# Attention and gated products on one core: chunks of 384 tokens instead of 256 from the second sequence on

## The chip, the core and the metric

The kernel runs on one core of one Trainium2 chip. The metric is the device time of one execution in microseconds (us), launch to end. Before the change three executions took 678.44, 678.51 and 681.38 us; their median is 678.51.

## The reference

Inputs are q, k and v of shape (4, 8, 768, 64), that is 4 sequences, 8 heads, 768 tokens and 64 columns, and three weights. Attention looks at the tokens nearer than 16 and at one summary for each block of 32 tokens; what it gives goes through two products whose results are multiplied, and a third.

```python
k_sum = k.reshape(B, H, nb, 32, D).max(axis=3)
v_sum = v.reshape(B, H, nb, 32, D).mean(axis=3)
scores_l = np.where(abs(i - j) < 16, scale * q @ k.T, -1e9)
scores_s = scale * q @ k_sum.T + np.log(32)
a = softmax(concatenate([scores_l, scores_s]))
x = (a @ concatenate([v, v_sum])).reshape(3072, 512)
out = ((x @ w_a) * (x @ w_b)) @ w_out        # 512 -> 1536 -> 512, all float32
```

## The kernel before

**Tiling.** The 3072 tokens are cut into 12 chunks of 256 (CH), three to a sequence. The 1536 hidden columns are cut into 12 slices f of 128. An *item* is one slice for one chunk: 24 up products (12 for "a" into one half of a bank, 12 for "b" into the other; 4 pieces of 128 rows times three hi/lo parts, since each float32 operand is held as a high and a low part of type fp32r), a chain that forms a times b and splits it, and 6 down products of 128x512 that add into two output banks. The chain of an item is: ACT copies "a" to g (L1013), DVE multiplies into the bank (L1016), ACT casts to the high part gh (L1018), DVE subtracts for the low part gl (L1021). Items alternate between banks h0 and h1 and between two copies of g, gh and gl. The down products with gh and gl of an item (L1070, L1071) are ranked half an item after its up products, so they stand in PE's order behind the up products of the next item.

**Stages.** Chunks 0 and 1 run side by side while the weights are loaded and converted; that part has its own attention code (`first_attention`). FILL is 2: the attention of chunk 2 is made during that stage. From there on one chunk after the other runs through its 12 items, and the attention of chunk u+2 is put in behind the last item of chunk u, so that it is made while PE works on chunk u+1. Attention goes by tiles of 128 queries: 32 score products into two banks, then on DVE scale and mask (L642), maxima and sums, on ACT the exponentials (L662), on GpSimd (POOL) the division, 12 transposes of 32x32 blocks on DVE (L736), 32 value products (L750), and a split of the result into the chunk's inputs x hi (ACT, L758) and x lo (DVE, L761). There is one score buffer `s`, one transposed buffer `pt` and one pair of value windows vw0, vw1. From chunk 4 on a tile's value products are held back (`lead`) and stand in front of the next tile's scores. The first chunk of each later sequence also brings `prep_keys` (keys transposed, block maxima) and `prep_values` (block means by GpSimd, which go through a part of S0 into the value windows).

**Order.** Nothing is put on an engine as it is written. Each step is given to `Work` with an engine, a rank, an estimated time and the names that it reads and writes; `emit` then plays the program through by these estimates, and on each engine takes the ready step of the lowest rank. The chain's steps have rank 0 (CHAIN), attention of the later chunks rank 6 (LATER), PE's attention products rank -1, loads about 100 on SP's queue. The table ORDER shifts some of the first 626 steps by their number; the change leaves it as it is.

**Banks and buffers.** h0, h1: up products. o0, o1: output of even and odd rows of a chunk (o2, o3 for chunk 1). c0, c1, and o2, o3 in turn: scores and values. At the end of a chunk ACT copies o0 and DVE copies o1 into S0 (L1076, L1082), and SP sends each to DRAM. In names of rows, numbers behind an underscore are only serial numbers of buffers.

## Time and profile before

| | |
|---|---|
| median of 3 executions | 678.51 us |
| the profiled execution, its own time | 678.28 us |
| its span in the trace | 676.5 us |
| mean granted clock of TensorE | 0.999 |
| L736, block transposes on DVE into `pt` | 228, busy 99.4 us |

The profile is of one execution. "Busy" is the time in which an engine has an instruction under way; PE is the matrix engine's products and PEld its weight loads, which run beside them. A group's row gives line, engine, operation, output and inputs, shape, count, then busy time and the mean duration of one in ns, then the idle time in front of such instructions and what ended it. A timeline row gives the start, the duration from the first to the last of a run of like instructions, the engine, the line and, in brackets, the wait and its releaser. SPq is the time in which SP issues transfers; DMA rows are the transfers themselves.

### The profile page before, as it was taken

How to read it: one execution, taken by the hardware profiler on the slowest of the kernel's cores; microseconds unless marked ns; L12 is line 12 of the kernel's file. 1: busy time of each engine (PE TensorE's matmuls, PEld its weight loads, DVE VectorE, ACT ScalarE, POOL GpSimd, SP SyncE). 2: the span in 40 equal slices, each digit the busy share in tenths (PEclk: the TensorE clock that was granted, in tenths of full speed). 3: DMA queues.
4: the chain of work that ended last, by engine and by line, in shares of the span. 5: the costliest groups of instructions: out<-in, count | busy, mean ns of one | idle time of the engine just before them, and what ended most of it. 6: DMA issues, size and time to landing. Idle time of an engine off the chain costs nothing.

```text
span 676.5 us, 15121 instructions
## 1 busy us (share of the span) xinstructions
PE 657.0 (97%) x5988; PEld 620.7 (92%) x5988; DVE 434.4 (64%) x989; ACT 255.4 (38%) x797; POOL 186.8 (28%) x231
## 2 busy tenths in 40 slices
PE   6889999999999999999999999999999999999997
PEld 4679989899999999999999999999999999999996
DVE  4799999996757768777665776762772762322222
ACT  4996665533323333234332332332332432211211
POOL 6678979851533310413110101110110110000000
PEclk9999999999999999999999999999999999999999
DMA  9999863266224135532311330310310100000000
GB/s 226 264 284 238 266 169 126 41 137 137 67 78 112 49 56 103 96 61 80 57 25 28 75 57 15 77 25 1 87 25 1 56 22 1 33 1 1 32 1 32
DMA packets 155087, 54.84 MB, mean 81 GB/s; under 512 B 132472, under 2 KB 148088, under 8 KB 155016
## 3 DMA queue, kind: packets, MB, share of 16 engines
q1 hardware_dynamic: 154872, 53.74, 33.5%
q8 instruction: 47, 0.77, 0.5%
q14 instruction: 24, 0.20, 0.1%
q10 hardware_dynamic: 144, 0.13, 0.1%
HBM read 47.12 MB, written 6.29 MB: 79 GB/s over the span
## 4 chain that ended last, share of the span: by engine, by line
PE 77%; DVE 11%; SPq 3%; ACT 3%; issue 2%; DMA 2%; POOL 1%; DVEq 0%; ACTq 0%; POOLq 0%
PE h L987 47%; PE o L1031 23%; SPq L260 3%; DVE c L339 2%; PE c L750 2%; PE c L617 2%; PE o L750 1%; DVE pt L736 1%; ACT s L662 1%; DVE space L345 1%; PE o L617 1%; DVE S L345 1%; DVE space L332 1%; DMA space<-in_v_dram 1%; DVE S L332 1%
## 5 line engine op out<-in xcount | busy, mean ns | idle before, releaser
L987 PEld LDWEIGHTS h<-x,w 128*128 128x128 f32 x3456 | 405.0, 192 | 6.8 <-DVE x L761 0.6
L987 PE MATMUL h<-x,w 128*128 128x256 f32 x3456 | 406.7, 275 | 0.3 <-DVE x L761 0.3
L1016 DVE TENSOR_TENSOR h<-h,g 128x256 f32<-128x256 f32 x144 | 61.9, 430 | 148.9 <-ACT g L1013 147.6
L1031 PE MATMUL o<-w,gh 128*128 128x512 f32 x576 | 151.8, 386 | 1.4 <-ACT gh L1018 1.3
L1013 ACT COPY g<-h 128x256 f32<-128x256 f32 x144 | 53.6, 372 | 256.4 <-PE h L987 256.3
L1031 PEld LDWEIGHTS o<-w,gh 128*128 128x128 f32 x576 | 103.6, 197 | 12.1 <-ACT gh L1018 2.6
L692 POOL TENSOR_TENSOR s<-s,nml 128x512 f32<-128x512 f32 x40 | 41.6, 1041 | 233.1 <-DVE nml L677 232.6
L736 DVE STREAM_TRANSPOSE pt<-s 32x256 f32<-32x256 f32 x228 | 99.4, 436 | 7.1 <-POOL s L692 2.0
L1031 PE MATMUL o<-w,gl 128*128 128x512 f32 x288 | 86.3, 381 | 0.0
L1021 DVE TENSOR_TENSOR gl<-h,gh 128x256 fp32r<-128x256 f32 x144 | 60.4, 419 | 30.6 <-ACT gh L1018 29.3
L662 ACT ACTIVATE s<-s,nml 128x128 f32<-128x128 f32 x160 | 62.2, 391 | 44.9 <-DVE nml L650 44.9
L1018 ACT CAST gh<-h 128x256 fp32r<-128x256 f32 x144 | 53.5, 371 | 65.3 <-DVE h L1016 65.1
L1031 PEld LDWEIGHTS o<-w,gl 128*128 128x128 f32 x288 | 55.9, 196 | 6.1 <-issue 0.3
L545 POOL TENSOR_TENSOR S<-S 96x64 f32<-96x64 f32 (+3 forms) x54 | 35.2, 651 | 41.6 <-DMA S<-in_v_dram 30.7
L324 ACT ACTIVATE c<-raw 128x512 f32<-128x512 f32 x36 | 26.9, 748 | 13.1 <-DVE S L332 6.6
L662 ACT ACTIVATION_READ_ACCUMULATOR s<-s,nml 128x1 f32 x160 | 30.1, 188 | 0.0
L382 POOL TENSOR_TENSOR space<-space,w 128x1024 f32<-128x1024 f32 (+1 forms) x14 | 26.8, 1915 | 8.8 <-ACT w L377 6.6
L671 DVE TENSOR_SCALAR nml<-nml 128x4 f32<-128x4 f32 x40 | 9.6, 243 | 28.4 <-ACT s L662 28.4
L388 POOL TENSOR_TENSOR w<-space 128x1024 fp32r<-128x1024 f32 (+1 forms) x14 | 26.7, 1912 | 1.0
L650 DVE TENSOR_REDUCE nml<-s 128x4 f32<-128x512 f32 x40 | 25.3, 667 | 0.0
L444 POOL COPY kT<-ksum 128x144 f32<-128x144 f32 x16 | 4.7, 308 | 62.8 <-DVE ksum L522 48.0
L382 POOL TENSOR_TENSOR S<-S,w 128x512 f32<-128x512 f32 (+1 forms) x11 | 17.4, 1582 | 6.4 <-ACT w L377 6.4
(109 smaller groups left out, 460.6 us busy)
## 6 DMA issues: line engine op xcount, KB each, us to landing
raw<-in_moe_w_a_dram SPq DMA_DIRECT2D x12, 512.0 KB
raw<-in_moe_w_b_dram SPq DMA_DIRECT2D x12, 512.0 KB
raw<-in_moe_w_out_dram SPq DMA_DIRECT2D x12, 512.0 KB
out_dram<-S SPq DMA_DIRECT2D x23, 256.0 KB
qin<-in_q_dram SPq DMA_DIRECT2D x160, 32.0 KB
S<-in_v_dram SPq DMA_DIRECT2D x24, 192.0 KB
vw<-in_v_dram SPq DMA_DIRECT2D x18, 192.0 KB
kin<-in_k_dram SPq DMA_DIRECT2D x24, 100.0 KB
```

The costliest lines, as they stand in the source:

```text
L324: nc.scalar.activation(bank["c0"], high[:, :, 1].bitcast(F32), AF.Prelu, scale=2.0**-112, alpha=-(2.0**32))
L382: lambda ms=ms, f8=f8: nc.gpsimd.tensor_tensor(out=f8, in0=f8, in1=parted(0)[:, ms].bitcast(F32), op=ALU.subtract),
L545: lambda: nc.gpsimd.tensor_tensor(out=out, in0=i0, in1=i1, op=ALU.add),
L662: lambda h=h, c=c, sums=sums: nc.scalar.activation(s[h][:, c, :], x[h][:, c, :], AF.Exp, bias=m[:, 0, h, c : c + 1], scale=1.0, accum_out= ...
L692: lambda h=h, r=r: nc.gpsimd.tensor_tensor(out=s[h], in0=s[h], in1=r[:, :, None].broadcast_to([P, NP, P]), op=ALU.mult,),
L736: lambda js=js, qs=qs: nc.vector.transpose(out=pv[js, :, qs], in_=sv[qs, :, js]),
L987: nc.tensor.matmul(ps, w[:, c, part, :], x[xpart][:, c, :].rearrange("p (a b) -> p b a", a=G), start=(i == 0), stop=(i == n - 1),)
L1013: act(CHAIN, 0.38, [hk], [gk], lambda: nc.scalar.copy(out=g, in_=pa))
L1016: lambda: nc.vector.tensor_tensor(out=pa, in0=pb, in1=g, op=ALU.mult),
L1018: act(CHAIN, 0.41, [hk], [ghk], lambda: nc.scalar.copy(out=gh, in_=pa))
L1021: lambda: nc.vector.tensor_tensor(out=gl, in0=pa, in1=gh.bitcast(F32), op=ALU.subtract),
L1031: nc.tensor.matmul(bank[ok[j]], (gh if first else gl)[:, j::G], w[:, :, part, :].rearrange("p (z a) n -> p z n a", a=2), start=(f == 0 and ...
```

## The change

Sequence 0 keeps its three chunks of 256 tokens. The other three sequences are cut into two chunks of 384 each (`WIDE` = 3 tiles of 128), so there are 9 chunks and 108 items in place of 144; 36 of the items are those of chunks 0 to 2 and 72 are wide. With it go:

- From chunk 2 on "a" has bank h0 and "b" bank h1, each up to 384 columns wide, and there is one g, gh and gl of 384 columns. Chunks 0 and 1 keep the old item.
- The down products of a wide item are nine, into o0, o1 and o2. Value products go to o3, scores always to c0 and c1.
- All chunks' inputs lie in one tile `x` of nine pieces; the low part of chunk 3 lies in `late`, in S0's place. Tokens within a piece are read in an order that takes one from each half of 64 in turn.
- Output copies go through two pieces of S1 in place of S0; the third bank's copy uses the first piece again.
- Queries are loaded tile by tile (16 loads of 32x4x32 each) in place of chunk by chunk. Block means go from `vm` straight into the value windows, 8 transfers for each of the two windows.
- Key rows of the second half go through the same buffer `kin` as those of the first, but for sequence 1.
- The last item's "b" products are ranked ahead of a part of the down products before.

```diff
+    WIDE = 3
+    chunks = [(0, t, G) for t in range(0, S // P, G)]
+    chunks += [(b, t, WIDE) for b in range(1, B) for t in range(0, S // P, WIDE)]
+    NU = len(chunks)
...
-    xs = [[sb([P, NP, CH], f"x{i}_{p}", F32R) for p in range(2)] for i in range(2)]
-    gs = [sb([P, CH], f"g{i}") for i in range(2)]
+    xt = sb([P, 9, NP, P], "x", F32R)
+    gt, ght, glt = sb([P, 2 * CH], "g"), sb([P, WIDE * P], "gh", F32R), sb([P, WIDE * P], "gl", F32R)
...
+    def homes_of(u):
+        n = chunks[u][2]
+        if u <= FILL:
+            return [[f"X{u % 2 * 2 * G + p * G + i}" for i in range(n)] for p in range(2)]
+        if u % 2:
+            return [[f"X{6 + i}" for i in range(n)], [f"S0.{i}" for i in range(n)]]
+        return [[f"X{p * WIDE + i}" for i in range(n)] for p in range(2)]
...
     def prep_keys(b):
-        more = ["done12"], ["S1.2", "S1.3"]
+        if b == 1:
+            work.add("-", 0, 0, 0, (), ["S0.0", "S0.1"], lambda: None)
         for c in range(NP):
-            kw = kins[c % 2]
+            own = b == 1 and c % 2
+            kw = spaces["S0"][:, : S + 32] if own else kin
...
     def prep_values(b):
-            for h in range(4):
-                load(
-                    99, 6.0, 20, [pk, vk], [f"{vk}.{hg}.{h}"],
-                    vs[:, 4 * hg + h, :], vm[h * NS : (h + 1) * NS, :],
-                )
...
         def split():
+            act(
+                CHAIN if u > FILL else rank, 0.6, [bk], [hk] + (also if i == 2 else []),
+                lambda: nc.scalar.copy(out=home(0), in_=y),
+            )
             dve(
-                rank, 0.6, [bk, xk + "h"], [xk + "l"],
+                CHAIN if u > FILL else rank, 0.6, [bk, hk], [lk] + (also if i == 0 else []),
...
     def attention(u):
-        if u > FILL:
-            banks, vbank = [["c0", "c1"], ["o2", "o3"]], ["c0", "o2"]
+        banks, vbank = ["c0", "c1"], ["c0", "c1"] if u == FILL else ["o3"] * n
...
         def bring(i):
-                    load(97, 49.0, 100, sums, [VK[3 + e]], vbuf[e][r0 : r0 + NS], vsums[b])
+                    for h in range(H):
+                        load(
+                            97, 6.0, 20, [f"vm{h // 4}"],
+                            [f"v{3 + e}.{h}"] + [VK[3 + e]] * (u == FILL + 1),
+                            vbuf[e][r0 : r0 + NS, h, :],
+                            vm[h % 4 * NS : (h % 4 + 1) * NS, h // 4, :],
+                        )
         def begin(i):
+            if u > FILL:
+                for c in range(NP):
+                    keys += blocks(
+                        98, f"q{(t0 + i) % 2}.{c}", qin[:, c, place(i)], q, b, c, (t0 + i) * P, (),
+                        fill if u == FILL + 1 and i < 2 else (),
+                    )
...
     def up(nm, f, u, ps):
-                    x[xpart][:, c, :].rearrange("p (a b) -> p b a", a=G),
+                    inputs_of(u, xpart)[:, :, c].rearrange("p g (a b) -> p g b a", a=2),
...
     def item(n, u, f):
+        ok = [f"o{2 * (u == 1) + j}" for j in range(m)]
+            W = m * P
+            pa, pb, g, gh, gl = bank["h0"][:, :W], bank["h1"][:, :W], gt[:, :W], ght[:, :W], glt[:, :W]
+            for nm, ps, hk in (("a", pa, "h0"), ("b", pb, "h1")):
+                pe(
+                    n - (1.45 if n == total - 1 and nm == "b" else 0), 12 * (0.112 if m == 2 else 0.163), xk + weight_key(f, nm), [hk],
+                    lambda nm=nm, ps=ps: up(nm, f, u, ps),
+                )
+            act(CHAIN, 0.13 + W / 1030, ["h0"], ["g0", "g1"], lambda: nc.scalar.copy(out=g, in_=pa))
...
-                        bank[ok[j]], (gh if first else gl)[:, j::G],
+                        bank[ok[j]], (gh if first else gl)[:, j * P : (j + 1) * P],
...
         if f == NF - 1:
-            for j in range(2):
-                ob, key = slot("S0", j)
+            for j in range(m):
+                ob, key = slot("S1", j % 2)
```

Three places show how the order of the instructions changes. The first is **PE in the later chunks**. A row has the line, the operation, output and inputs, the shape, what it waits for, and a count; h are the up banks, o the output banks, x the inputs, w a piece of the weights. Before, around one run of down products:

```order
L987 MATMUL h0_75<-x1_0_171,w15_1477 128x256
L1031 MATMUL o0_71<-w14_1384,gh1_176 128x512 [waits Activation_49]
L1031 MATMUL o0_71<-w14_1384,gh1_176 128x512
L1031 MATMUL o1_72<-w14_1384,gh1_176 128x512 x2
L1031 MATMUL o0_71<-w14_1384,gl1_178 128x512 [waits DVE_49]
L1031 MATMUL o1_72<-w14_1384,gl1_178 128x512
L987 MATMUL h1_76<-x1_0_171,w16_1558 128x256
```

And now:

```order
L1024 MATMUL h1_76<-x_169,w5_802 128x384 x12
L1024 MATMUL h0_75<-x_169,w6_871 128x384 [waits Activation_49]
L1024 MATMUL h0_75<-x_169,w6_871 128x384 x11
L1095 MATMUL o0_71<-w5_802,gh_171 128x512 [waits Activation_49]
L1095 MATMUL o0_71<-w5_802,gh_171 128x512
L1095 MATMUL o1_72<-w5_802,gh_171 128x512 x2
L1095 MATMUL o2_73<-w5_802,gh_171 128x512 x2
L1095 MATMUL o0_71<-w5_802,gl_172 128x512 [waits DVE_49]
L1095 MATMUL o1_72<-w5_802,gl_172 128x512
L1095 MATMUL o2_73<-w5_802,gl_172 128x512
L1024 MATMUL h1_76<-x_169,w6_871 128x384 x12
```

Before, all 24 up products of the next item stood between an item's up products and its down products. Now the 12 "a" products of the next item stand there, and they wait for ACT's copy of the bank's last "a"; the next item's "b" follows the down products.

The second is **DVE near the end of chunk 2**, where the inputs of chunk 3 are finished. s is the score buffer, pt the transposed one, c0, c1, o2 and o3 are banks. Before, the end of the second and last tile of chunk 3:

```order
L736 STREAM_TRANSPOSE pt_164<-s_163 32x8x32 x5
L761 TENSOR_TENSOR x1_1_172<-c0_77,x1_0_171 128x4x128 [waits Activation_49]
L1016 TENSOR_TENSOR h0_75<-h0_75,g0_173 128x256 [waits Activation_49]
L1021 TENSOR_TENSOR gl0_177<-h0_75,gh0_175 128x256 [waits Activation_49]
L1016 TENSOR_TENSOR h1_76<-h1_76,g1_174 128x256 [waits Activation_49]
L1021 TENSOR_TENSOR gl1_178<-h1_76,gh1_176 128x256 [waits Activation_49]
L761 TENSOR_TENSOR x1_1_172<-o2_73,x1_0_171 128x4x128 [waits Activation_49]
L642 SCALAR_TENSOR_TENSOR s_163<-c0_77,mask_86 128x512 [waits DVE_49,PE_49]
```

And now, the end of the third tile:

```order
L750 STREAM_TRANSPOSE pt_164<-s_163 32x8x32 x6
L1081 TENSOR_TENSOR h1_76<-h1_76,g_170 128x256 [waits PE_49,Activation_49]
L656 SCALAR_TENSOR_TENSOR s_163<-c0_77,mask_86 128x512 [waits DVE_49]
L1086 TENSOR_TENSOR gl_172<-h1_76,gh_171 128x256 [waits Activation_49]
L656 SCALAR_TENSOR_TENSOR s_163<-c1_78,mask_86 128x512
L664 TENSOR_REDUCE nml1_179<-s_163 128x4 [waits DVE_49]
L788 TENSOR_TENSOR late_2351<-o3_74,x_169 128x4x64x2 [waits Activation_49]
L1146 COPY S1_181<-o1_72 128x512 [waits PE_49]
```

Before, two tiles were finished here and both splits stood ahead of the next tile's scores; now the third tile's transposes end about one item before the chunk's end, the first tile of chunk 4 has begun on `s`, and the last split stands beside the copy of the bank o1.

The third is **ACT at the change from one wide chunk to the next**. g, gh are the chain's, S1 takes the output copies, x the inputs. Before, at such a place:

```order
L1076 COPY S0_186<-o0_71 128x512 [waits DMAHW2_49,PE_49]
L1013 COPY g0_173<-h0_75 128x256 [waits PE_49,Activation_49]
L1018 CAST gh0_175<-h0_75 128x256 [waits DVE_49]
L1013 COPY g1_174<-h1_76 128x256 [waits PE_49,Activation_49]
L1018 CAST gh1_176<-h1_76 128x256 [waits DVE_49]
```

And now:

```order
L1078 COPY g_170<-h0_75 128x384 [waits PE_49,Activation_49]
L1140 COPY S1_181<-o0_71 128x512 [waits DMAHW4_49,PE_49]
L1083 CAST gh_171<-h1_76 128x384 [waits DVE_49]
L1078 COPY g_170<-h0_75 128x384 [waits PE_49,Activation_49]
L1140 COPY S1_181<-o2_73 128x512 [waits DMAHW7_49,Activation_49]
L1083 CAST gh_171<-h1_76 128x384 [waits DVE_49,PE_49]
L784 CAST x_169<-o3_74 128x4x64x2 [waits PE_49]
```

One copy of an output bank on ACT became two; the second waits for the transfer that empties the piece of S1, and the cast gh of the next item stands behind it.

199 lines of the change are left out of this document (112 added, 87 removed).

## The prediction, made before the changed kernel ran

> **What bounds the kernel now.** First the page, for the busy shares and the slices; then the windows, for where TensorE (PE) waits; then the chain of waits, for what one step costs.
>
> ```profile
> span 676.5 us, 15121 instructions
> ...
> PE 657.0 (97%) x5988; PEld 620.7 (92%) x5988; DVE 434.4 (64%) x989; ACT 255.4 (38%) x797; POOL 186.8 (28%) x231
> ...
> PEclk9999999999999999999999999999999999999999
> ...
> GB/s 226 264 284 238 266 169 126 41 137 137 67 78 112 49 56 103 96 61 80 57 25 28 75 57 15 77 25 1 87 25 1 56 22 1 33 1 1 32 1 32
> ```
>
> ```profile
> core 0: us, PE busy (x) PEld busy (x) DVE busy (x) ACT busy (x) POOL busy (x), PEclk, DMA share, GB/s
> ...
> 160.00:210.00 50.00, 49.43 (x486) 46.63 (x485) 32.71 (x73) 18.84 (x73) 20.31 (x29) 1.00 0.39 92
> 210.00:260.00 50.00, 50.00 (x515) 47.53 (x515) 36.38 (x88) 15.96 (x58) 11.07 (x14) 1.00 0.27 58
> ...
> 560.00:660.00 100.00, 100.00 (x777) 96.71 (x776) 23.82 (x54) 20.59 (x54) 0.00 (x0) 1.00 0.03 12
> ```
>
> PE is the bound: it fills every window from 210 to 660 us at the full granted clock, while VectorE (DVE) has a quarter of its time free. So an edit helps only where it shortens PE's own work, and hurts where PE has to wait. The chain shows the price of one item (one slice of 128 hidden columns for one chunk):
>
> ```profile
> 571.25 2.68 PE h L987 x24
> 573.93 1.30 PE o L1031 x6
> 575.23 2.68 PE h L987 x24
> ```
>
> An item of 256 tokens is 24 up products and 6 down products, 2.68 + 1.30 = 3.98 us: 111.7 ns for 256 columns, 217 ns for 512. Twice the columns cost 1.95 times as much, so something small is paid per product and not per column.
>
> **The change, part by part.** The sum is made against the profiled execution: 678.28 us, of which the span is 676.5; it lies 0.03% under the median of the runs, 678.51.
>
> *Wider up products.* Chunks 3 to 11 of 256 tokens (108 items) become 6 chunks of 384 (72 items). Columns stay the same; 2592 products of 256 become 1728 of 384. No row has 384 columns. Upper end: the straight line between the two rows, 111.7 + (217 - 111.7)/2 = 164.4 ns. Lower end: the row of 512 shows four products in 0.87 us and two in 0.43 (403.36 to 404.23, to 404.66), 215 ns inside a run, of which three quarters are 161.3.
>
> ```profile
> 403.36 1.03 PE L1031 MATMUL o<-w,gh 128*128 128x512 f32 x4
> 404.23 0.59 PE L1031 MATMUL o<-w,gl 128*128 128x512 f32 x2
> 404.66 2.84 PE L987 MATMUL h<-x,w 128*128 128x256 f32 x24
> ```
>
> I take three quarters of 217, 163.0. One and a half of the old item's up work is 4.02 us, the new one 24 x 0.163 = 3.91: 0.11 us less in each of 72 items, **-7.8 us** (-10.7 at 161.3, -5.3 at 164.4). I stay below the line because a weight load stands before each product, and the row of loads is busy as long as the products themselves at 256 columns but not at 512:
>
> ```profile
> L987 PE MATMUL h<-x,w 128*128 128x256 f32 x3456 | 406.7, 275 | 0.3 <-DVE x L761 0.3
> L987 PEld LDWEIGHTS h<-x,w 128*128 128x128 f32 x3456 | 405.0, 192 | 6.8 <-DVE x L761 0.6 <-DVE gl L1021 0.3 <-issue 0.2
> L1031 PE MATMUL o<-w,gh 128*128 128x512 f32 x576 | 151.8, 386 | 1.4 <-ACT gh L1018 1.3
> L1031 PEld LDWEIGHTS o<-w,gh 128*128 128x128 f32 x576 | 103.6, 197 | 12.1 <-ACT gh L1018 2.6 <-ACT x L758 1.5 <-issue 1.4
> ```
>
> [...] Down products, score and value products are as many as before, in the same shapes: 0.
>
> *One bank for each half.* Before, items alternated between two banks and two copies of g, gh and gl, so the chain from the products to the down products had a whole item to finish. Now "a" lands in h0, "b" in h1, and while the chain of one item runs, PE has only the "a" half of the next: 12 x 0.163 = 1.96 us. The end of the program shows the chain with nothing before it:
>
> ```profile
> 669.33 1.03 PE L1031 MATMUL o<-w,gh 128*128 128x512 f32 x4
> 669.58 0.37 ACT L1013 COPY g<-h 128x256 f32<-128x256 f32 x1 [2.74 <-PE h L987]
> ...
> 669.99 0.43 DVE L1016 TENSOR_TENSOR h<-h,g 128x256 f32<-128x256 f32 x1 [2.69 <-ACT g L1013]
> ...
> 670.45 0.37 ACT L1018 CAST gh<-h 128x256 fp32r<-128x256 f32 x1 [0.50 <-DVE h L1016]
> ...
> 670.88 0.32 PEld L1031 LDWEIGHTS o<-w,gh 128*128 128x128 f32 x2 [0.48 <-ACT gh L1018]
> ```
>
> From the end of the up products (669.33) ACT starts 0.25 later; multiply to down products is 670.88 - 669.99 = 0.89. The copy g now falls under the "b" half. Widths grow by half; the 512 rows give the slope:
>
> ```profile
> L1082 DVE COPY S<-o 128x512 f32<-128x512 f32 x11 | 7.4, 677 | 1.4 <-PE o L1031 1.3
> L1076 ACT COPY S<-o 128x512 f32<-128x512 f32 x11 | 6.5, 590 | 13.8 <-PE o L1031 13.8
> ```
>
> Multiply 0.43 to 0.55, cast 0.37 to 0.48, so 0.25 + 0.89 + 0.12 + 0.11 = 1.37 of the 1.96 us. 0.59 us are left for other work in front on DVE and ACT; the longest such instruction is about 0.7, the size of the copy of 512 columns. I take **0**, with 0 to +3 us for the range. The cover that hides it is the next "a" half; where it fails, PE waits at the first down product.
>
> *Three tiles for the first wide chunk.* Chunk 2 keeps 256 tokens, and while PE works on it (48 us), the attention of chunk 3 has to be done, now three tiles instead of two. They go one after the other, since there is one score buffer and one transposed buffer.
>
> ```profile
> 131.25 1.28 DVE L642 SCALAR_TENSOR_TENSOR s<-c,mask 128x512 f32<-128x512 f32 x2
> ...
> 144.98 0.44 DVE L736 STREAM_TRANSPOSE S<-s 32x256 f32<-32x256 f32 x1
> ...
> 161.84 0.69 DVE L642 SCALAR_TENSOR_TENSOR s<-c,mask 128x512 f32<-128x512 f32 x1 [0.17 <-PE c L617]
> ...
> 178.28 1.27 DVE L642 SCALAR_TENSOR_TENSOR s<-o,mask 128x512 f32<-128x512 f32 x2
> ```
>
> ```profile
> 151.24 5.52 PE L987 MATMUL h<-x,w 128*128 128x256 f32 x48
> ...
> 201.09 1.15 PE L750 MATMUL o<-pt,vw 128*64 128x64 f32 x32
> 202.18 1.10 PE L617 MATMUL c<-kT,qT 64*64 64x128 f32 x32
> ...
> 205.91 5.52 PE L987 MATMUL h<-x,w 128*128 128x256 f32 x48
> ```
>
> A tile takes 14.2 us at the quickest (131.25 to 145.42, the end of its last transpose) and 16.4 in this very stage (161.84 to 178.28). The first tile's scores stay where they were, about 161.8. Three tiles end their transposes between 161.8 + 3 x 14.2 = 204.4 and 161.8 + 3 x 16.4 = 211.0; values (1.1) and their split on ACT and DVE (about 1.3) follow, so chunk 3 can start between 206.8 and 213.4. It started at 205.91; one more value and one more score product stand ahead of it now (2.3 us, taken from later, not lost), so up to 208.2 costs nothing. The loss is 0 to 5.2 us; I take **+3.5**, nearer the 16.4 of this stage. What is late then is PE's first wide "a", behind the split of the third tile.
>
> *Copies out of three banks.* The third bank's copy goes into the same piece of S1 as the first's, so it waits on ACT until that transfer has left, and "gh" casts queue behind it. First copy 0.25 + 0.59, issue 0.45, and a landing of about 2 us for a small transfer (the chain's row) and 256 KB more at the 284 GB/s of the page's best slice, 0.9: 4.2; then 0.59 again: 4.8 us. The order puts three halves (5.9 us) before the next chunk's down products, and o2 is the last of them. So there is 1 us of cover, five times; SP's queue, where query loads of 0.54 us each stand (below), can use it up. I take **+1.0** in all, range 0 to 5.
>
> ```profile
> 187.00 1.97 DMA S<-S
> ```
>
> *The end.* The last "b" half is moved before one run of 3 down products (0.65 us), and its chain of 1.37 then shows 0.7 where before 0.25 showed (669.33 + 1.30 = 670.63, to 670.88): **+0.5**.
>
> *Loads.* Query loads become twice as many of half the size (288 for 144 in the last three sequences), and the block means go straight to their places in 16 small transfers in place of 8 and 2. SP issues them in line:
>
> ```profile
> 164.10 8.70 SPq L260 DMA_DIRECT2D qin<-in_q_dram  x16
> ...
> 184.33 3.40 SPq L260 DMA_DIRECT2D S<-S  x4
> ...
> 191.97 1.04 PE L750 MATMUL c<-pt,vw 128*64 128x64 f32 x28 [0.36 <-DMA vw<-S]
> ```
>
> That is 0.54 us a query load and 0.85 a small transfer. A sequence (24 wide items of 5.87, 141 us) has 96 x 0.54 + 16 x 0.85 = 65 us of these, under half of SP's time: 0, since the loads lie beside PE's work, except in chunk 2's stage (second rival), where that cover is short.
>
> Sum: -7.8 + 3.5 + 1.0 + 0.5 = -2.8, so 678.28 - 2.8 = **675.5 us**.
>
> **The rivals.**
> *The hand-over costs nothing.* If DVE's tiles run at 14.2 us, the third is ready before PE is: -7.8 + 1.0 + 0.5 = -6.3, 672 us. For it: no PE wait between chunks after 210 us. Against: 16.4 measured in this stage.
> *The means come late.* The block means of the values reach the first of the three tiles through SP. From the reload of the value window on, which waits for chunk 2's own value products just ahead of 151.24, SP's order has 32 query loads and 16 means before the last mean: 32 x 0.54 + 16 x 0.85 = 31 us, so 182 and a landing of 2. The first tile's values stand in PE's order behind 13 halves of 1.34, 6 runs of down products of 1.30 and 3 score products of 1.1, 28.5 us, so at 179.8. PE would wait 4 us, and the next tiles shift behind it: +4, so +1.2 and 679.5 us. For it: PE waited there before too (0.36 us, for the same means). Against: a query load of half the size may issue faster than 0.54.
> *The cover is too short (slower).* If DVE or ACT hold up the chain by more than 0.59 us, every wide item loses the excess. Beyond 0.1 us a mean item in the 60 items that have attention beside them, 6 us, the kernel is slower than before by about 0.5%; at 0.25 us it is 15 - 2.8 = +12, 690 us. For it: the gate is two engines long and in order, and "gh" sits behind exponentials. Against: its instructions are chosen first by the planner, and DVE's load per chunk does not rise.
> *The products do not get cheaper.* The moving operand is read with halves 64 columns apart, where before it was 128 (x) and 256 (w); no row shows 64. An operand read in line is slower, four in 1.20 against 1.03 (first and last row of such a group), which on 282 us of up products would be +48. I give it little, because all distances shown run at full rate.
>
> ```profile
> 30.82 1.20 PE L604 MATMUL o<-space 128*128 128x512 f32 x4
> ```
>
> **How the numbers follow.** Forecast as summed (672.5 to 678.5): 0.46; no cost at the hand-over: 0.20; means late: 0.20; cover too short: 0.10; products not cheaper: 0.04. A measurement of this kernel can tell about 0.5%, 3.4 us. Faster by more: half of the first case and nearly all of the second, 0.42. Within: the rest of the first and nearly all of the third, 0.45. Slower: 0.13. The range is 670 to 682: at the top it takes in late means with 2.5 us of the other bounds, at the bottom a free hand-over with products at 162; what is left out is 161.3 without any cost (-10.7 + 0.5, 668) and a cover short by more than 0.1 us.
>
> **What would show it.** Up products of 384 in the chain: 12 in 1.96 us (right), 2.0 or more (no gain). PE idle before the first of them after 206 us: 3 us behind the third tile's split. PE's waits on "gh" in the wide chunks: under 1 us in all, or the cover is too short. Waits on ACT's copy of the third bank: up to 1 us. Wrong I am if PE is idle outside the hand-over by more than 3 us, or if 384 columns do not cost between 161 and 164.5 ns.

## The result and the profile after

The changed kernel took 696.46 us (median of 4 executions, 695.06 to 700.85), before 678.48: a ratio of 1.0265, 95% interval 1.021 to 1.0321. Forecast were 675.5 us, range 670 to 682. The profiled execution took 695.31 us. From its page, the lines that answer to those of before (span, busy time by engine, granted clock in 40 slices):

```profile
span 693.6 us, 13488 instructions
...
PE 656.6 (95%) x5124; PEld 607.4 (88%) x5124; DVE 434.6 (63%) x915; ACT 257.0 (37%) x728; POOL 186.4 (27%) x231
...
PEclk9999999999989999999999999999999999999999
```

PE is busy as long as before (657.0) in a longer span, although its products became cheaper. The chain of waits shows that they did:

```profile
363.20 1.94 PE o L1095 x9
365.15 3.90 PE h L1024 x24
```

A wide item is 5.84 us, one and a half of the old 3.98 is 5.97: 0.13 us less in each of 72 items, 9.4 us. What was lost is seen from the start of each chunk's first up product, taken from the trace. A tile of attention costs PE 2.32 us of products (half of 52.40, a chunk of before with two tiles, less 12 x 3.98). The third column is what was to be expected then: in chunk 2's stage what it took before and one tile more, in the wide chunks the products that the trace has between the two starts, at these prices. In chunk 3's stage these are 24 up products for each of 12 items, 11 runs of down products (the twelfth falls behind it) and three tiles; in chunk 4's, 12 items and four tiles (128 value and 128 score products), since one tile is made early there:

| us | before | to be expected | after |
|---|---|---|---|
| start of chunk 2 | 151.2 | 151.2 | 157.8 |
| chunk 2 to the start of chunk 3 | 54.7 | 57.0 | 68.1 |
| chunk 3 to the start of chunk 4 | | 75.1 | 77.4 |
| chunk 4 to the start of chunk 5 | | 79.4 | 83.5 |
| from the start of chunk 5 to the last product | | | 302.3 |
| last product of PE | 672.5 | | 689.0 |

So 6.6 us were lost before chunk 2, 11.1 in its stage, 2.3 in chunk 3's and 4.1 in chunk 4's, where the next sequence's keys and means are prepared. With the 9.4 won, that makes 672.5 - 9.4 + 24.1 = 687.2 of the 689.0; the other 1.8 lie behind the start of chunk 5. **Chunk 2's stage** on PE (timeline: start, us, line, then the wait):

```profile
157.76 0.38 PE L1024 MATMUL h<-x,w 128*128 128x256 f32 x1 [1.15 <-ACT x L784]
160.04 5.52 PE L1024 MATMUL h<-x,w 128*128 128x256 f32 x35 [1.90 <-DVE x L788]
...
191.71 0.33 PE L764 MATMUL o<-pt,vw 128*64 128x64 f32 x2 [0.66 <-DMA vw<-vm]
193.10 0.34 PE L764 MATMUL o<-pt,vw 128*64 128x64 f32 x4 [1.07 <-DMA vw<-vm]
...
197.33 4.42 PE L1024 MATMUL h<-x,w 128*128 128x256 f32 x24
...
202.88 2.84 PE L1024 MATMUL h<-x,w 128*128 128x256 f32 x24
```

PE waits for the splits of chunk 2, then, transfer by transfer, for the block means. And the 24 products behind the second wait take 4.42 us, where the same 24 take 2.84 a little later; the 35 behind the first take 5.52, where 35 at 111.7 ns are 3.9. The windows (length, then PE, PEld, DVE, ACT and POOL busy, then the granted clock, the DMA share and GB/s) say why:

```profile
155.00:160.00 5.00, 1.41 (x29) 1.08 (x29) 4.96 (x13) 1.48 (x2) 1.71 (x5) 0.95 0.26 44
160.00:165.00 5.00, 4.96 (x32) 4.96 (x33) 2.38 (x11) 0.58 (x2) 0.61 (x2) 0.71 1.00 258
...
185.00:190.00 5.00, 5.00 (x56) 4.42 (x58) 4.94 (x10) 1.17 (x5) 0.31 (x1) 1.00 0.20 30
190.00:195.00 5.00, 2.54 (x43) 1.71 (x34) 1.02 (x4) 2.00 (x11) 1.04 (x1) 0.86 0.17 47
195.00:200.00 5.00, 3.69 (x20) 3.25 (x19) 1.06 (x1) 1.72 (x5) 0.00 (x0) 0.50 0.16 25
200.00:205.00 5.00, 5.00 (x39) 4.84 (x38) 3.32 (x10) 0.79 (x3) 1.04 (x1) 0.96 0.49 102
```

Behind both thin stretches the granted clock is at half speed (0.50) for a while, in the trace from 159.5 us for 3.4 and from 193.6 us for 6.8, so the stalls of PE are paid for a second time here. PE was not idle all through the stretches ahead of them: it had work in 1.41 of the 4.5 us from 155 to 159.5 and in 1.72 of the 3.6 us from 190 to 193.6.

So the 11.1 us of this stage are waits and clock in nearly equal parts. PE's waits of over 0.1 us in it are 6.1 us: 1.9 for the split, 3.8 for the means, 0.4 for transposes. The clock, by the windows, took (0.05 + 0.29 + 0.14 + 0.50 + 0.04) x 5 = 5.1 us. Why the means were late is seen on SP's queue (issue of transfers) and on POOL:

```profile
163.91 6.30 SPq L284 DMA_DIRECT2D vw<-vm  x8
170.31 7.41 SPq L284 DMA_DIRECT2D qin<-in_q_dram  x14
177.83 1.05 SPq L284 DMA_DIRECT2D S<-in_v_dram  x2
178.94 10.17 SPq L284 DMA_DIRECT2D qin<-in_q_dram  x18
...
189.68 6.11 SPq L284 DMA_DIRECT2D vw<-vm  x8
```

```profile
169.79 0.31 POOL L466 COPY kT<-ksum 128x144 f32<-128x144 f32 x1 [7.65 <-DVE ksum L547]
...
181.46 3.00 POOL L564 TENSOR_TENSOR S<-S 96x512 f32<-96x512 f32 x4 [1.85 <-DMA S<-in_v_dram]
...
184.94 0.36 POOL L588 TENSOR_SCALAR vm<-vm 96x64 f32<-96x64 f32 x1
```

The second half of the means needs two more value loads. They stand on SP behind 8 mean transfers (0.79 us each) and 14 query loads (0.53 each), so POOL's sums end at 185.3; the transfers of these means then stand behind 18 more query loads until 189.7. Not all of this is SP's: the two loads go into the buffer that POOL's sums before them read, and these sums were through with it only at 173.06, since they stood behind a copy that waited 7.65 us for DVE. From there on SP's queue cost them 4.8 us, and the transfers of the means 4.4. **In chunk 4's stage** the same lateness takes another way (SP, POOL, DVE and PE):

```profile
317.52 2.59 SPq L284 DMA_DIRECT2D qin<-in_q_dram  x4
320.21 0.84 SPq L284 DMA_DIRECT2D S<-in_v_dram  x2
```

```profile
324.05 3.00 POOL L564 TENSOR_TENSOR S<-S 96x512 f32<-96x512 f32 x4 [15.29 <-DMA S<-in_v_dram]
...
327.98 2.04 POOL L706 TENSOR_TENSOR s<-s,nml 128x512 f32<-128x512 f32 x2
```

```profile
330.05 3.13 DVE L750 STREAM_TRANSPOSE pt<-s 32x256 f32<-32x256 f32 x7 [2.87 <-POOL s L706]
333.21 0.57 DVE L1081 TENSOR_TENSOR h<-h,g 128x384 f32<-128x384 f32 x1
```

```profile
334.34 1.56 PE L1095 MATMUL o<-w,gh 128*128 128x512 f32 x6 [1.59 <-ACT gh L1083]
```

The value loads come late, behind query loads; POOL's sums, which stand first in its queue, wait for them; the scaling of s stands behind them; DVE's transposes wait for s; and the chain's multiply, which needs nothing of all this, stands behind the transposes. So PE waits 1.59 us for gh, the largest piece of the 4.1 lost there. In these rows each queue is served in its order. In the view of waits (total, times, longest), the two kinds of wait:

```profile
PE o L764 <- DMA vw<-vm: 3.8, 6, 1.1
...
PE o L1095 <- ACT gh L1083: 3.2, 4, 1.6
```

Last, **the split** of the attention result, in before's groups and in the changed kernel's (count, busy us, mean ns):

```profile
L758 ACT CAST x<-c 128x512 fp32r<-128x512 f32 x11 | 6.5, 590 | 1.3 <-PE c L750 1.3
L761 DVE TENSOR_TENSOR x<-c,x 128x512 fp32r<-128x512 f32 x11 | 7.5, 685 | 0.3
```

```profile
L784 ACT CAST x<-o 128x512 fp32r<-128x512 f32 x20 | 21.6, 1078 | 32.8 <-PE o L764 23.1 <-PE h L1024 9.7
L788 DVE TENSOR_TENSOR x<-o,x 128x512 fp32r<-128x512 f32 x11 | 12.2, 1113 | 4.6 <-ACT x L784 4.6
```

The same 128x512 elements take 1.08 us on ACT in place of 0.59 and 1.11 on DVE in place of 0.69.

### The profile page after: what moved, and what is told of

Same layout as the page of the kernel before. It is cut to its first block, busy times and chain, and to the rows that moved or that the text cites. A ratio compares the mean times of both kernels' runs of the same rounds, so it can differ in the third digit from the quotient of the medians.

```text
span 693.6 us, 13488 instructions
## 1 busy us (share of the span) xinstructions
PE 656.6 (95%) x5124; PEld 607.4 (88%) x5124; DVE 434.6 (63%) x915; ACT 257.0 (37%) x728; POOL 186.4 (27%) x231
## 4 chain that ended last, share of the span: by engine, by line
PE 64%; SPq 12%; DMA 8%; DVE 7%; POOL 4%; ACT 3%; issue 2%; DVEq 0%; POOLq 0%; ACTq 0%
PE h L1024 39%; PE o L1095 20%; SPq L284 9%; SPq L313 3%; DMA raw<-in_moe_w_a_dram 3%; PE o L764 2%; DVE pt L750 2%; PE c L631 2%; DMA qin<-in_q_dram 2%; POOL w L412 2%; ACT s L676 1%; DMA space<-in_v_dram 1%; DMA raw<-in_moe_w_out_dram 1%; DMA space<-in_q_dram 1%; POOL space L406 1%
## 5 line engine op out<-in xcount | busy, mean ns | idle before, releaser
L1024 PE MATMUL h<-x,w 128*128 128x384 f32 (+1 forms) x2304 | 398.8, 309 | 3.9 <-DVE x L788 2.4
L1024 PEld LDWEIGHTS h<-x,w 128*128 128x128 f32 x2304 | 348.4, 192 | 10.1 <-DVE x L788 2.8
L1083 ACT CAST gh<-h 128x384 fp32r<-128x384 f32 (+1 forms) x84 | 39.1, 465 | 244.6 <-DVE h L1081 233.8
L1081 DVE TENSOR_TENSOR h<-h,g 128x384 f32<-128x384 f32 (+1 forms) x84 | 45.9, 546 | 127.5 <-PE h L1024 125.0
L750 DVE STREAM_TRANSPOSE pt<-s 32x256 f32<-32x256 f32 x228 | 99.4, 436 | 15.1 <-POOL s L706 11.1
L1024 PE MATMUL h<-late,w 128*128 128x384 f32 x288 | 94.0, 326 | 1.0 <-DVE late L788 1.0
L1086 DVE TENSOR_TENSOR gl<-h,gh 128x384 fp32r<-128x384 f32 (+1 forms) x84 | 45.0, 536 | 25.5 <-ACT gh L1083 22.1
L1078 ACT COPY g<-h 128x384 f32<-128x384 f32 (+1 forms) x84 | 38.8, 461 | 57.2 <-PE h L1024 56.7
L1024 PEld LDWEIGHTS h<-late,w 128*128 128x128 f32 x288 | 54.4, 189 | 2.2 <-DVE late L788 1.2
L564 POOL TENSOR_TENSOR S<-S 96x512 f32<-96x512 f32 (+3 forms) x42 | 31.3, 745 | 42.3 <-DMA S<-in_v_dram 40.2
L656 DVE SCALAR_TENSOR_TENSOR s<-c,mask 128x512 f32<-128x512 f32 x40 | 26.7, 683 | 23.0 <-PE c L631 22.9
```

What stands on the lines that cost most here:

```text
L750: lambda js=js, qs=qs: nc.vector.transpose(out=pv[js, :, qs], in_=sv[qs, :, js]),
L1024: nc.tensor.matmul(ps, w[:, c, part, :], inputs_of(u, xpart)[:, :, c].rearrange("p g (a b) -> p g b a", a=2), start=(i == 0), stop=(i == n ...
L1078: act(CHAIN, 0.13 + W / 1030, ["h0"], ["g0", "g1"], lambda: nc.scalar.copy(out=g, in_=pa))
L1081: lambda: nc.vector.tensor_tensor(out=pb, in0=pb, in1=g, op=ALU.mult),
L1083: act(CHAIN, 0.16 + W / 1030, ["h1"], [ghk], lambda: nc.scalar.copy(out=gh, in_=pb))
L1086: lambda: nc.vector.tensor_tensor(out=gl, in0=pb, in1=gh.bitcast(F32), op=ALU.subtract),
```

## The experiments

Four causes were suspected: the order of the first stage, which the change's estimates reshuffle (A); the longer split; SP's queue (S); and the third tile on DVE (D). Times are medians, with the ratio to the kernel of before on the same chip (678.3 to 679.0); the two stages are those of the profiled execution, which in e3, e6, e9 and e11 took 1.8 to 3.4 us longer than the median. e3 and e14 leave out a part of the work and serve as tests only.

| kernel | us | ratio, 95% | chunk 2 starts | its stage | chunk 4's stage |
|---|---|---|---|---|---|
| after | 696.5 | 1.021 to 1.032 | 157.8 | 68.1 | 83.5 |
| e1 estimates of before | 696.3 | 1.025 to 1.028 | 155.6 | 69.9 | 81.5 |
| e2 plain split | 695.1 | 1.021 to 1.025 | 154.6 | 68.2 | 86.8 |
| e3 early means | 696.6 | 1.024 to 1.030 | 157.4 | 73.6 | 82.8 |
| e4 = e1 + e2 | 690.1 | 1.015 to 1.018 | 153.6 | 68.8 | 82.1 |
| e5 = e4 + query pairs | 690.2 | 1.015 to 1.022 | 152.2 | 61.9 | 82.2 |
| e6 query pairs only | 694.9 | 1.023 to 1.028 | 159.9 | 64.0 | 84.9 |
| e7 = e5 + SP costs | 683.5 | 1.006 to 1.010 | 152.4 | 62.5 | 80.8 |
| e8 = e5 + nine means | 682.8 | 1.005 to 1.008 | 152.8 | 62.1 | 82.0 |
| e9 = e7 + e8 | 683.2 | 1.007 to 1.009 | 153.4 | 62.9 | 80.2 |
| e10 = e9, values first | 682.9 | 1.005 to 1.008 | 154.1 | 62.1 | 80.2 |
| e11 before, queries by tile | 691.3 | 1.014 to 1.020 | 154.4 | 65.4 | |
| e12 before, woven split | 681.5 | 1.003 to 1.006 | 154.7 | 54.9 | |
| e13 = e10, wide from sequence 2 | 677.2 | 0.996 to 0.998 | 153.5 | 53.1 | |
| e14 = e10, third tile cut | 674.7 | 0.991 to 0.995 | 153.9 | 56.8 | 80.2 |
| e15 = e10, estimates of the change | 681.9 | 1.002 to 1.006 | 155.3 | 62.0 | 80.2 |
| e16 = e10, split of the change | 687.9 | 1.010 to 1.014 | 155.1 | 63.4 | 80.2 |
| e17 = e13, values of sequence 1 late | 677.0 | 0.996 to 0.999 | 153.9 | 53.1 | |
| e18 = e13 again | 676.6 | 0.995 to 0.998 | 152.9 | 53.1 | |

**The first stage's order and the split (e1, e2, e4).**

```diff
-            pe(n, 2.685, xk + weight_key(f, "a") + weight_key(f, "b"), [hk], hidden)
+            pe(n, 2.76, xk + weight_key(f, "a") + weight_key(f, "b"), [hk], hidden)
...
-        pe(n - 0.5, 0.435 * m, [ghk] + weight_key(f, "o"), ok, lambda: down(True))
-        pe(n - 0.4, 0.2165 * m, [glk] + weight_key(f, "o"), ok, lambda: down(False))
+        pe(n - 0.5, 0.93 if u < FILL else 0.435 * m, [ghk] + weight_key(f, "o"), ok, lambda: down(True))
+        pe(n - 0.4, 0.46 if u < FILL else 0.2165 * m, [glk] + weight_key(f, "o"), ok, lambda: down(False))
```

> The changed kernel, but the planner's estimates for chunks 0 and 1 are again those of before (2.76, 0.93 and 0.46 us in place of 2.685, 0.87 and 0.433). With them the steps of that stage stand on every engine in the order of before, as far as the stage goes. Theory A (the shortened estimates reshuffled a stage whose order was set by a table of shifts, and that cost 6.5 us): the first up product of chunk 2 comes at 151 to 154 us in place of 157.8, and the time falls by 6 to 9 us from 696, to 687 to 690. Rival B (the stage is later because of the longer splits of x, 1.08 us in place of 0.6, or of buffers that are shared now): it comes at 156 or later, and the time falls by less than 2 us.

```diff
-            y = ps.rearrange("p c (b a) -> p c b a", a=2)
+            y = ps
...
-                return inputs_of(u, part)[:, i].rearrange("p c (a b) -> p c b a", a=2)
+                return inputs_of(u, part)[:, i]
...
+        return out[row : row + P, :].rearrange("(a b) d -> b a d", a=2)
```

> The changed kernel, but the split writes x in line, as before, and no longer one token from each half; the rows come out in another order then, and the output transfers put them right. The rows of the split (L784 on ACT 1.08 us, L788 on DVE 1.1 us) should go back to 0.6 and 0.68. Theory: PE's waits for the splits (4.6 us in all in the view of waits, at the starts of chunks 2, 3, 5 and in the last attention) fall by about 0.8 us at each of 4 places, and the time by 2 to 4 us. Rival: something else ends at the same moment, and the time stays within 1 us, or rises because transfers whose rows go to two places take longer.

> The estimates of before for chunks 0 and 1 and the split in line, together. If both theories hold and the two losses lie at different places, the time falls by the sum of the two, 8 to 12 us, to 684 to 688. If they are one loss seen twice, no further than the larger of the two alone.

e1 gained nothing. Chunk 2 started 2.2 us earlier, less than theory A wanted, and its stage took 1.8 us longer. e2 gained 1.4 us, less than the 2 to 4 of its theory. Together they gained 6 to 7, less than the 8 to 12 of the sum. e4 had the start at 153.6, 4.2 us earlier, and a stage of 68.8, 0.7 longer, so there most of the earlier start was kept. In e2 it was lost further on: its chunk 4's stage took 86.8 us, in e4 82.1. That is 4.7 of the 5.0 us between the two, although their edit differs only in estimates for chunks 0 and 1. So a small change of the planned order can move some 5 us in a stage far behind it, and one such gain alone shows little.

**The means (e3).**

```diff
-                            97, 6.0, 20, [f"vm{h // 4}"],
+                            97, 6.0, 20, [f"vm{h // 4 if b > 1 else 0}"],
...
-                            vm[h % 4 * NS : (h % 4 + 1) * NS, h // 4, :],
+                            vm[h % 4 * NS : (h % 4 + 1) * NS, h // 4 if b > 1 else 0, :],
```

> The changed kernel, but in sequence 1 the second four heads get the block means of the first four (so their own means are left out of the result), which are ready some 20 us earlier. Theory M (the means come late and hold up everything behind them): PE's waits for the value windows (3.8 us) go, and so does the low granted clock behind them (4.42 us for an item's up products in place of 2.84): the time falls by 5 to 7 us, to 689 to 691. Rival T (the third tile is late in any case, since DVE needs its time for three tiles): the time falls by less than 2 us and PE waits that much longer at the start of chunk 3.

PE no longer waited for the means, and the time stayed, as rival T had it, but not for its reason. Neither theory named what came in their place (SP, then DVE, POOL and DVE again):

```profile
180.61 13.98 SPq L284 DMA_DIRECT2D qin<-in_q_dram  x26
...
197.37 16.24 SPq L284 DMA_DIRECT2D qin<-in_q_dram  x31
213.65 0.43 SPq L284 DMA_DIRECT2D S<-in_v_dram  x1
```

```profile
196.23 0.71 DVE L976 STREAM_TRANSPOSE qT<-qin 128x512 f32<-128x512 f32 x1 [4.18 <-DMA qin<-in_q_dram]
...
220.34 0.43 DVE L750 STREAM_TRANSPOSE pt<-s 32x256 f32<-32x256 f32 x1 [5.86 <-POOL s L706]
220.71 0.39 DVE L1081 TENSOR_TENSOR h<-h,g 128x256 f32<-128x256 f32 x1
```

```profile
216.35 1.28 POOL L564 TENSOR_TENSOR S<-S 96x512 f32<-96x512 f32 x1 [16.54 <-DMA S<-in_v_dram]
```

First the queries themselves are late, then again a value load behind 31 query loads. Whatever is taken off this queue, the next thing in it is late: this is what made SP the suspect. In this execution PE's waits for gh rose from 3.2 to 9.9 us.

**SP's queue (e5 to e11).** e5 loads queries for two tiles at a time, 48 loads to a sequence in place of 96, e6 does only that:

```diff
...
-                    keys += blocks(
-                        98, f"q{(t0 + i) % 2}.{c}", qin[:, c, place(i)], q, b, c, (t0 + i) * P, (),
-                        fill if u == FILL + 1 and i < 2 else (),
-                    )
+            if u > FILL and (t0 + i) % 2 == 0:
+                for c in range(NP):
+                    blocks(98, f"qin.{c}", qin[:, c, :], q, b, c, (t0 + i) * P)
```

> e4 (690.1 us), with the queries loaded for two tiles at a time: 48 loads to a sequence in place of 96, as many as before the change. Theory S (SP's queue, in which each query load stands for 0.52 us, delays the value loads behind it; POOL, whose sums stand ahead of the scaling of s, waits for them; then the transposes, the value products and PE are late): the waits of POOL for S<-in_v (15 us and 16 us ahead of 209.8 and 319.1) end earlier, chunk 2 takes 60 us or less from its first up product to that of chunk 3 (68.9 in e4), chunk 4 less than 80 (82.2), and the time falls by 7 to 11 us, to 679 to 683. Rival D (three tiles are too many for DVE in this stage, however the loads come): chunk 2 still takes over 66 us and the time falls by less than 3 us.

> The changed kernel as it is (estimates and split of the change), with only the queries loaded for two tiles at a time. Theory S: from 696 to 685 to 690 (chunk 2 and chunk 4 get shorter, the late start of chunk 2 at 157.8 stays). Rival D: within 3 us of 696.

By the time both missed theory S: e5 stayed at e4's, e6 gained 1.5 us. In e5 chunk 2's stage fell by 6.9 us, which rival D excludes, and all of it was lost again in chunk 5's, which took 84.1 us in place of 77.0. In e6 chunk 2's stage fell by 4.1 us, but it began 2.1 later, and chunk 5's took 81.3 in place of 77.6. SP and DVE of e5:

```profile
424.56 7.89 SPq L284 DMA_DIRECT2D vw<-vm  x10
432.56 8.60 SPq L284 DMA_DIRECT2D qin<-in_q_dram  x16
```

```profile
442.72 0.71 DVE L972 STREAM_TRANSPOSE qT<-qin 128x512 f32<-128x512 f32 x1 [4.83 <-DMA qin<-in_q_dram]
443.36 1.24 DVE L664 TENSOR_REDUCE nml<-s 128x4 f32<-128x512 f32 x2
444.51 0.56 DVE L1080 TENSOR_TENSOR h<-h,g 128x384 f32<-128x384 f32 x1
```

Ten means at 0.79 us stood ahead of the queries; the transpose of the queries waited, and the multiply of the chain behind it. Half of the loss is the clock again: 0.56 and 0.76 in the windows of 5 us from 445 and 450, so 3.4 us (mean granted clock of the run 0.990, of e8 0.995). e7 tells the planner what a load costs on SP, e8 takes seven of the 16 mean transfers away:

```diff
...
+        takes = 0.45 if len(work.ops) < 780 else 0.78 if kb == 6.0 else 0.52
```

```diff
...
+                load(
+                    97, 49.0, 100, VS[:H], VS[H:] + [VK[4]] * (u == FILL + 1),
+                    vbuf[1][32 : 32 + NS], vbuf[0][WIN : WIN + NS],
+                )
```

> e5, with the planner told from chunk 2's attention on what a load takes on SP (0.52 us, and 0.78 for a block mean, in place of 0.45 for all). Theory S says that what is left of the waits comes from loads that the planner thinks earlier than they are: then waits of POOL and PE get shorter and the time is 1 to 3 us under e5. If it is the same within 1 us, the number of loads was all, or the queue is no longer late.

> e5, with the block means brought by 8 small transfers and one of all heads from the first window to the second, in place of 16 small ones: 7 x 0.78 = 5.5 us less of SP in a sequence, at the price of one more landing (about 2 us) ahead of the first tile's values. Theory S: chunk 2's and chunk 4's stages get shorter by another 1 to 3 us against e5. If SP is no longer what is late, no gain, or a loss up to 2 us by the added landing.

> e8 with the planner's SP costs of e7. If e7 and e8 took away the same stall (the query loads of chunk 5's stage that came 4.8 us late in e5 behind ten block means), the two do not add: 681 to 683. If they took away different waits, 676 to 679.

Each brought 7 us more than e5 and not the 1 to 3 expected, since each removed the whole stall in chunk 5's stage (77.1 in both); together (e9) they brought no more, as the first case of e9 had it. From e4 to e7 or e8, taking the loads back in these two steps is worth 6 to 7 us. e10 ranks all value loads ahead of the queries:

```diff
-                    (93, 100)[b > 1], 197.0, 150, (), [keys[i % 2]],
+                    93, 197.0, 150, (), [keys[i % 2]],
```

> e9, with the value loads of sequences 2 and 3 ranked ahead of the query loads on SP, as those of sequence 1 are. Theory S: in chunk 4's stage POOL's sums are then done before the softmax needs POOL (in e8 they end at 312.2 and 316.5, after the sums of rows were ready at 311.8 and 313.9), the multiply of the chain no longer stands behind transposes that wait for POOL, and chunk 4 takes 77 to 79 us in place of 82: 3 to 5 us under e9. If chunk 4 stays at 82, POOL's sums are not what holds it up.

It missed: chunk 4's stage stayed at 80.2, as in e9. With the four tiles that are made in it, 79.4 us are its products alone, so nearly nothing was left to win there. The converse was tried on the kernel of before, with only its queries loaded tile by tile:

```diff
-            qk += blocks(98, f"qin.{c}", qin[:, c, :], q, b, c, r * CH, ["done4"] if u == FILL else ())
...
+                    keys += blocks(
+                        98, f"q{i}.{c}", qin[:, c, i * P : (i + 1) * P], q, b, c, (t0 + i) * P, (),
```

> The kernel of before with one part of the change alone: queries loaded tile by tile, 96 loads to a sequence in place of 48. Theory S: 16 more loads of 0.52 us in each stage of 52 us make SP late there too: 681 to 688, with POOL, DVE and then PE waiting behind late loads in the first stage or stages. Rival: SP has room for them in this kernel (about 8 us more in 52), and the time stays within 1.5 us of before; then the loads are only harmful together with the 16 block means and the third tile.

It rose by 10 to 14 us (13 by the medians), more than expected. Its six executions took 686.4 to 693.6 us: the two shortest had a mean granted clock of 0.997 and 0.995, the others 0.985 to 0.988, so by an estimate from these times the waits alone cost some 8 us, and the clock behind them up to 7 more. Its rows (SP, POOL, PE) are those of the changed kernel over again:

```profile
175.20 15.96 SPq L260 DMA_DIRECT2D qin<-in_q_dram  x32
191.26 7.45 SPq L260 DMA_DIRECT2D S<-in_v_dram  x3
```

```profile
194.96 3.41 POOL L545 TENSOR_TENSOR S<-S 96x512 f32<-96x512 f32 x5 [6.93 <-DMA S<-in_v_dram]
```

```profile
205.39 0.48 PE L750 MATMUL c<-pt,vw 128*64 128x64 f32 x4 [3.24 <-DMA vw<-S]
```

Loading the queries tile by tile, which makes twice as many loads of half the size and asks for them at another point of the order, is enough, without wide chunks, a third tile or the direct means. Which of the two counts was not tested apart.

**The split alone and taken back (e12, e16), the estimates taken back (e15).**

```diff
-                y[:, :, P * (t % G) : P * (t % G + 1)]
+                y[:, :, P * (t % G) : P * (t % G + 1)].rearrange("p c (a b) -> p c b a", a=2)
...
-                    x[xpart][:, c, :].rearrange("p (a b) -> p b a", a=G),
+                    x[xpart][:, c, :].rearrange("p (g a b) -> p g b a", g=G, a=2),
...
-                        bank[ok[j]], (gh if first else gl)[:, j::G],
+                        bank[ok[j]], (gh if first else gl)[:, j * P : (j + 1) * P],
```

> The kernel of before with another part alone: the split writes one token from each half of a tile in turn, and the products read it back, as in the change; so the operand of the up products is read 64 columns apart. The split should take 1.08 us on ACT and 1.1 on DVE in place of 0.6 and 0.68 in all 24 tiles. If it is hidden outside the first stage and the hand-over to chunk 2: 679 to 682. If the planner's order, which knows 0.6, comes apart in the first stage as it did between e1 and e4 (2 us at chunk 2's start, 2 us of waits behind it): 682 to 685. The up products stay at 111.7 ns in either case.

> e10, with the change's split (one token from each half in turn; 1.08 and 1.1 us in place of 0.6 and 0.68). In the kernel of before that part alone cost 3.2 us, all of it before chunk 2. Here it should cost 3 to 5 us, since the splits at the starts of chunks 2 and 3 are waited for: 686 to 688. Under 2 us, if the hand-over waits for something else.

> e10, with the change's own estimates for chunks 0 and 1 again (2.685, 0.87, 0.433). Alone (e1) putting them back was worth nothing in the end, since what was won at the start of chunk 2 was lost behind SP. If the first stage is worth what chunk 2's start shows (157.8 against 152 to 154), the time rises by 3 to 6 us over e10, to 686 to 689. If the stage behind it takes it up as slack, less than 1.5 us.

The split alone cost the kernel of before 3.2 us (2 to 4 by the interval), all of it before chunk 2, and its rows were those of the changed kernel:

```profile
L762 ACT CAST x<-c 128x512 fp32r<-128x512 f32 x11 | 11.9, 1085 | 1.6 <-PE c L750 1.6
```

Taken back in e16 it cost 4 to 5 us over e10. The split of the change writes x alternately, element by element, to two places 64 columns apart. Its price on 128x512 in e12 was 0.5 us on ACT (1085 ns in place of 590) and 0.4 on DVE (1112 in place of 685); what makes such a write slower is not shown. e15 went against theory A: with the change's estimates put back the time was 1 to 2 us lower, within the noise of the two intervals, and not 3 to 6 higher. The order of the first stage was changed, but in e1 and e15 that cost nothing that shows in the time; between e2 and e4 the same edit moved 5 us, in chunk 4's stage.

**The third tile (e14, e13, e17, e18).**

```diff
-            for j in kb:
+            for j in kb[:1] if u == FILL + 1 and t == 2 else kb:
```

> e10, with 8 of the 12 block transposes of the third tile of chunk 3 left out (part of that tile's weights is old data then): 8 x 0.45 = 3.6 us less of DVE just ahead of the hand-over. If DVE is what the third tile waits for (theory D), the start of chunk 3 comes 3 to 4 us earlier (2.5 us of waits for pt go) and the time falls by 2.5 to 4.5 us to 678.5 to 680.5. If a load or POOL is late there, it falls by less than 1 us.

Taking 3.6 us of DVE work out shortened the stage by 5.3 us, to what was to be expected, and the time by 8 to 9, more than forecast. In e10 the wait was there by name (view of waits):

```profile
PE o L765 <- DVE pt L751: 2.5, 1, 2.5
```

With the waits for the split around it, PE's waits in e10's stage are 3.7 us; in e14 none is over 0.1. The clock makes up most of the rest: in the windows of 5 us from 210 to 225 it is 0.89, 0.50 and 0.93 in e10, which is 3.4 us in this stage and chunk 3's, and 1.00 in e14 (mean granted clock of the two runs 0.993 and 0.999).

e13 gives sequence 1 chunks of 256 as well, so that chunk 2's stage has two tiles again:

```diff
-    chunks = [(0, t, G) for t in range(0, S // P, G)]
-    chunks += [(b, t, WIDE) for b in range(1, B) for t in range(0, S // P, WIDE)]
+    chunks = [(b, t, G) for b in range(2) for t in range(0, S // P, G)]
+    chunks += [(b, t, WIDE) for b in range(2, B) for t in range(0, S // P, WIDE)]
```

> e10, but sequence 1 keeps chunks of 256 as well; only sequences 2 and 3 have wide chunks. What wide chunks save is 1.56 us each by the traces (12 x (1.5 x 3.98 - 5.84)), so two less cost 3.1 us; but chunk 2's stage has two tiles to prepare again, not three. Theory D (what is left, some 5 us at chunk 2's stage, is the third tile in the stage in which SP, POOL and DVE have most to do): chunk 2 takes 55 to 57 us in place of 62, the hand-over to the first wide chunk comes later and costs 0 to 3: 678 to 682. If the loss of 5 us only moves to the later hand-over, 685 to 687.

> e13 once more, for the interval, beside the same runs of the kernel before: 0.993 to 1.0 of it. By the traces it should be 1 to 3 us faster (PE ends at 670.6 us in place of 672.5).

> e13 (677.2 us), with the value loads of sequence 1 ranked behind its queries, as before the change; its stages have two tiles again, so its means are not needed early. In e13 chunk 2 starts at 153.5, in the kernel of before at 151.2; where it comes apart, about 138 us, POOL's sums start earlier than they did and one small DVE step of 0.18 us takes 2.06 beside them. If the early value loads cause that, chunk 2 starts at 151 to 152 and the time falls by 1 to 2 us, to 675 to 676. If not, the time stays within 1 us of e13, or rises where the means are late again.

e13 is faster than the kernel of before, by 0.2 to 0.5% in both measurements (677.2 and 676.6). Its hand-over to the first wide chunk, with three tiles in a stage of 256 tokens, takes 55.4 us, where its products alone are 54.7 (12 x 3.98 and three tiles), and PE has no wait of over 0.1 us in it: next to nothing is lost. e17 missed: chunk 2 started no earlier.

## Why the prediction was wrong

- **"Loads ... 0, since the loads lie beside PE's work"** is the step that failed. The count was right (96 loads at 0.52, 16 means at 0.79), and the prediction itself said that the cover was short in chunk 2's stage, but its sum still took 0. It weighed SP's time against a whole sequence: summed from SP's rows, the issues fill 57% of the time from 157.8 to 541.5 us, but 91% of chunk 2's stage (62% before). And what counts is what stands behind them: value loads, hence POOL's sums, hence the means, the scaling of s, the transposes and the chain's multiply. Measured: 6 to 7 us when the loads are taken back (e4 to e7 or e8), 10 to 14 when queries by tile are added to the kernel of before (e11).
- **The rival "the means come late"** had the right place (the first tile's values wait for vw, forecast 4 us, measured 3.8 in the view of waits) and too small a price: it stopped at the first wait. e3 shows that this wait was only one of several that one late queue hands out.
- **The clock had no term.** The prediction saw PE at the full granted clock before and priced every wait at its length. In the changed kernel the half clock behind the waits took another 5.1 us, in e10 3.4.
- **"Three tiles for the first wide chunk", +3.5**: the mechanism was right, the upper bound of 5.2 too low. With SP relieved (e8 to e10) the stage takes 62.1 to 62.9 where 57.0 were to be expected, so 5.1 to 5.9; in e10 the waits are 3.7 of that, near the forecast, and the clock behind them, partly in chunk 3's stage, comes on top. With DVE's work cut (e14) the stage takes 56.8. In the changed kernel itself 11.1 were lost there, but only 0.4 of PE's waits were for transposes: the means and the split came first.
- **No term at all** was made for the split, although the diff shows its access patterns: 0.4 to 0.5 us more on ACT and on DVE for each tile, worth 3.2 us in the kernel of before and 4 to 5 in e16.
- **"Wider up products", -7.8**: the sign and the size were right; with the down products, nine in 1.94, it was -9.4. 24 up products of 384 took 3.90, 162.5 each, where 163.0 was taken. The rival of the operand stride is out: 64 columns apart cost the products nothing (in e12 3456 of them were busy for 406.7 us, as before). Two slips in the working change nothing: 217 / 111.7 is 1.94, and 282 x (1.20 / 1.03 - 1) is 47. That the 1.20 comes from reading in line was the author's estimate; no run shows it apart.
- **"One bank for each half", 0 to +3**: PE's waits for gh in chunks 2 to 8 were 3.2 us in the changed kernel, 0.6 of it at the end of the program, where under 1 was the sign of being right; the longest, 1.59, is not from the chain's own length but from the late transposes in front of its multiply. The rival "cover too short" was right that other work in front on DVE decides, and wrong that it would be the same for every item.
- **"Copies out of three banks", +1.0**: one wait of 0.4 us for the copy; 0.6 less than the term. **"The end", +0.5**: from the three down products at 685.41 (0.65 us) to the next at 686.81 it is 0.75 us, where 0.7 was forecast; right.
- The first stage was taken as unchanged. Its order did change with three estimates, and chunk 2 began 6.6 us later; but e15 and e1 leave for the order itself nothing that shows in the time. The late start came in part from the split (e12: 3.5 us); the rest is not settled.

All of these together are seen in e14, which has the estimates, the split and the loads taken back and leaves out eight transposes: 674.7 us, where 675.5 were forecast. That the two are so close is partly luck, since the forecast has +3.5 for the third tile and e14 pays next to nothing for it.

What stays open: chunk 2 started 1 to 3 us later than in the kernel of before in every repaired version (e5, e7 to e10, e13, e14); e17 excluded one cause of that and named none. The shares of the causes do not add up exactly either, since each depends on the order that the planner makes of the rest.

## What to carry to other kernels

When an edit makes more or smaller transfers, look at what stands behind them in the issuing queue, and follow that to the first engine that needs it and to what stands behind *there*; the share of the queue's time over a long stretch says nothing of its fullest stage. Here waits that left PE work in 1.72 of 3.6 us had a granted clock of 0.50 behind them for 6.8 us, so they cost more than their length. A planner that costs a load at 0.45 us where it takes 0.52 to 0.79 lays out an order that cannot be kept, and where each queue is served in its order, as in the rows of chunk 4's stage, the chain on the critical path waits for work that it doesn't need (there 1.59 us for gh, behind sums that waited 15.29 us for a load). Read the access patterns in a diff as well as the shapes: the same 65536 elements cost 1.08 us or 0.59 on ACT.

## What the runs showed of the hardware

- A transfer of 24x64 from one place of SBUF to another took SP 0.79 us to issue (8 in 6.30), a query load of 32x4x32 0.51 (mean of 256), one of 32x8x32 before 0.54 (mean of 128): half the size took 0.03 us off a query load, so in these runs the number of loads counted on that queue and their size hardly.
- Waits of PE cost more than their length: behind 3.6 us in which PE had work in 1.72, the granted clock was 0.50 for 6.8 us, and 24 products took 4.42 us in place of 2.84.
- Up products that read their operand 64 columns apart took as long as before (e12: 3456 busy for 406.7 us in both; 162.5 ns for 384 columns in the changed kernel), while a write with the same pattern took 1.8 times as long on ACT (1085 ns, before 590) and 1.6 times on DVE (1112, before 685), which also reads x in that pattern.
